# Gated linear attention and a mixture of experts on one core: the scans' additive operand in PSUM, the k product on GpSimd, one causal select in four by predicated copy, carried states without zero blocks

## The chip, the cores and the metric

The kernel runs on one core of a Trainium2 chip. Its engines are TensorE (PE in the profile; PEld is its weight load), VectorE (DVE), ScalarE (ACT), GpSimd (POOL) and SyncE (SP), which here issues most of the DMAs. The working memory is SBUF, 128 partitions wide; TensorE writes its products into PSUM, from which DVE and ACT read. The metric is the time of one execution on the device in microseconds; lower is better.

## The reference

Four sequences of 768 positions, with 8 heads of 48 channels, go through a gated linear attention in float32. Its output, 3072 tokens of 384 features, goes to a layer of 8 experts with a fixed capacity of 384 tokens each.

```python
# q, k, v, alpha: (4, 8, 768, 48), alpha in 0.8 .. 1.0
for t in range(S):
    state = alpha[:, :, t, :, None] * state + np.einsum('bhd,bhe->bhde', k[:, :, t], v[:, :, t])
    y[:, :, t] = np.einsum('bhd,bhde->bhe', q[:, :, t], state)
...
logits = x @ w_gate                      # x: y as (3072, 384)
order = np.argsort(-logits.flatten())    # greedy, at most cap = 384 tokens an expert
...
    h = np.maximum(x[mask] @ w1[e], 0.0)
    out[mask] = h @ w2[e]
```

## The kernel before

*Tiles.* The recurrence is computed in chunks of 128 positions, six to a sequence, 24 chunks in all. A step `s` of the attention loop takes four chunks (a group `g`) of one pair of heads (`p`); `s = 4*g + p`, so there are 24 steps, numbered 0 to 23. A tile has 128 partitions: rows 0 to 47 hold the channels of the first head, rows 64 to 111 those of the second. Along the free axis lie the four chunks `u` of 128 positions.

*One step.* DVE makes from the decays alpha two cumulative products with scans. Line 221 runs backwards through the step's four chunks: `sc[t] = alpha[t]*sc[t+1] + d1r[t]`. The alpha tile has a zero at each chunk's border (every 129th element), and `d1r` a one, so the product starts anew for each chunk. Line 222 takes the reciprocals of the four whole-chunk products into `d1f`, and line 224 scans forward with these as starting values: `ga`. Then `kh = k*sc` (line 229, DVE) and `qh = q*ga` (line 235, GpSimd). TensorE transposes `kh` (241) and ACT copies it as `kn` (243). The scores are `kh` against `qh`, for each chunk and head a matmul over the 64 rows of that head (250), into two PSUM tiles, `s0` and `s1`, with two buffers each. ACT copies each to SBUF (258), and GpSimd zeroes there what lies above the diagonal (259): two copies and two selects a step. TensorE forms the state that each chunk adds (269, PSUM bank `st`). The carry (273 to 289) goes chunk by chunk: ACT writes the state before the chunk, scaled by the chunk's decay, into a tile `sb` (282), and DVE adds the chunk's state (289), or copies it where a sequence begins (287). `sb` is block diagonal, 128x128: one 64x64 block for each head, the other two blocks zero from the beginning, and ACT writes one instruction for each block. The outputs are, for each chunk, one 128x128 matmul with `sb` (296) and two with the masked scores and v (302), all into the PSUM tile `y`. ACT copies it as `yt` (310). Two steps later the routing logits follow from it (315, also in the bank `st`), which DVE copies (318, where p is 0) or adds (320). With the last pair of a group comes a transpose and the table work of the first routing choice (`first_choice`, lines 347 to 365), a dozen small DVE instructions.

*The loop.* In iteration `s` the program names: the loads of step s+3, keys, scores and causal select of s, logits of s-2, states and carry of s, scans and products of s+2, outputs of s-1 and their copy. A scheduler then orders each engine's instructions. SP issues the loads of a step in a fixed order, alpha, k, q, v. Each of these has four buffers. The v tile of step s+3 takes the buffer of step s-1, which is free when the outputs of s-1 are done, and what stands behind that load on SP waits with it.

*After the attention* come the rest of the routing, a search for each expert's threshold by counting matmuls (551) and comparisons (503), gathers of each expert's tokens, and the two layers of each expert, each product in three terms of a split into two rounded parts (lines 719 to 789). The change does not touch their code.

```python
        if s + 2 < NS:
            decay(s + 2)
            scale_k(s + 2)
            scale_q(s + 2, nc.vector if s == 0 else nc.gpsimd)
        if s and s <= NS:
            mix(outputs(s - 1))
            emit(s - 1)
```

The first two steps are prepared before the loop by `first` (398), in halves.

## Time and profile before

| | us |
|---|---|
| three runs | 517.44, 517.86, 510.74; median 517.44 |
| the profiled execution, its own time | 513.45 |
| its span, first to last instruction | 511.7 |
| attention loop, from the first scan of the loop on (14 to 149) | 135 |
| end of the attention (149 to 160) | 11 |
| search for the thresholds of routing (160 to 200) | 40 |
| experts (200 to 511) | 311 |

| engine | busy us of the span | share |
|---|---|---|
| PE | 419.5 | 82% |
| DVE | 337.2 | 66% |
| POOL | 275.6 | 54% |
| ACT | 229.7 | 45% |

The mean clock granted to TensorE was 0.931 of full speed. Rows of groups read: line, engine, operation, output and inputs, shapes, count, then busy time in us and mean of one in ns, then the idle time of the engine just ahead of these instructions and what ended it. Rows of a stretch give the busy time of each engine in it with the number of instructions. Instructions of one engine overlap a little at their ends, so durations add up to somewhat more than busy time.

### The profile page before, as it was taken

The numbers are of one execution on the slowest core, as the hardware profiler recorded it, in microseconds if no ns is written. First come the engines' busy times: TensorE is split into PE (matmuls) and PEld (weight loads), VectorE is DVE, ScalarE is ACT, GpSimd is POOL, SyncE is SP. The second block draws the span as 40 slices with busy tenths as digits, with TensorE's granted clock in tenths as the row PEclk, the third lists the DMA queues.
The fourth block names the chain that finished last, engine by engine and source line by source line (L and its number), as shares of the span: only waits on it lengthen the run. The fifth ranks groups of instructions, "written<-read, shape, count | busy, mean of one in ns | idle before, by whom it ended". The sixth has DMA issues, their size and how long they took to land.

```text
span 511.7 us, 10469 instructions
## 1 busy us (share of the span) xinstructions
PE 419.5 (82%) x3982; PEld 365.8 (71%) x3982; DVE 337.2 (66%) x868; ACT 229.7 (45%) x524; POOL 275.6 (54%) x277
## 2 busy tenths in 40 slices
PE   6777877887878767985887867988967899999994
PEld 3555666666666646975786766877966789999994
DVE  7999897889743567687686796594684774121210
ACT  2676677677875433141322332242332245464521
POOL 2756755475630057274535455357548367978632
PEclk9999999889999957997988989897989899999998
DMA  8655556465503563170251161082152162620001
GB/s 257 206 169 174 168 164 169 162 176 176 167 1 122 216 205 122 44 252 0 83 212 46 51 243 47 1 277 63 60 188 94 30 217 68 250 91 26 31 17 46
DMA packets 44593, 65.17 MB, mean 127 GB/s; under 512 B 3328, under 2 KB 26880, under 8 KB 44544
## 3 DMA queue, kind: packets, MB, share of 16 engines
q1 hardware_dynamic: 38304, 50.35, 30.6%
q0 software_dynamic: 3072, 9.44, 5.7%
q10 hardware_dynamic: 3168, 4.72, 2.5%
q8 instruction: 31, 0.51, 0.4%
q14 instruction: 18, 0.15, 0.1%
HBM read 55.06 MB, written 9.44 MB: 126 GB/s over the span
## 4 chain that ended last, share of the span: by engine, by line
PE 44%; DVE 33%; DMA 9%; issue 6%; ACT 3%; POOL 1%; another core or an unknown queue 1%; SPq 1%; POOLq 0%; ACTq 0%; DVEq 0%
PE y L778 15%; PE h L758 14%; PE rt L551 5%; DVE sc L221 5%; DVE nd L563 4%; DVE cmp L503 4%; DMA al<-in_alpha_dram 4%; DVE ga L224 3%; PE xt L742 2%; DMA x_dram<-xg 2%; DMA raw_k<-in_k_dram 2%; PE y L302 1%; DVE st L289 1%; ACT sb L282 1%; PE y L296 1%
## 5 line engine op out<-in xcount | busy, mean ns | idle before, releaser
L724 POOL TENSOR_TENSOR wlo<-w1r,whi 128x384 fp32r<-128x384 f32 x64 | 71.2, 1115 | 85.7 <-ACT whi L719 85.4
L762 ACT ACTIVATE hh<-h 128x384 fp32r<-128x384 f32 x64 | 31.5, 492 | 107.6 <-PE h L758 105.3
L259 POOL TENSOR_SCALAR_AFFINE_SELECT sm<-sm 128x512 f32<-128x512 f32 x48 | 42.4, 902 | 59.8 <-ACT sm L258 59.8
L763 DVE SCALAR_TENSOR_TENSOR hl<-h,hh 128x384 fp32r<-128x384 f32 x64 | 35.4, 553 | 57.4 <-ACT hh L762 54.7
L778 PE MATMUL y<-whi,hh 128*128 128x384 f32 x192 | 70.3, 366 | 0.0
L778 PE MATMUL y<-wlo,hh 128*128 128x384 f32 x192 | 69.7, 363 | 0.0
L778 PE MATMUL y<-whi,hl 128*128 128x384 f32 x192 | 69.1, 361 | 0.0
L719 ACT ACTIVATE whi<-w1r 128x384 fp32r<-128x384 f32 x64 | 32.8, 522 | 80.0 <-PE y L778 69.5
L725 POOL TENSOR_TENSOR wlo<-w2r,whi 128x384 fp32r<-128x384 f32 x64 | 65.8, 1031 | 3.9 <-ACT whi L720 3.7
L282 ACT ACTIVATE sb<-st,sc 64x48 f32<-64x48 f32 x160 | 53.1, 332 | 29.5 <-DVE st L289 14.2
L699 POOL DMA_INDIRECT xr<-x_dram,idx x24 | 28.6, 1193 | 48.4 <-DVE val L630 31.2
L551 PE MATMUL rt<-o,cmp 128*128 128x8 bf16 x816 | 32.7, 175 | 25.0 <-DVE cmp L503 17.6
L551 PEld LDWEIGHTS <-cmp 128*128 128x128 bf16 x816 | 30.5, 118 | 31.7 <-DVE cmp L503 20.5
L758 PE MATMUL h<-xh,whi 128*128 128x384 f32 x192 | 48.1, 353 | 5.0 <-DVE hl L763 5.0
L758 PE MATMUL h<-xh,wlo 128*128 128x384 f32 x192 | 50.6, 363 | 0.0
L758 PE MATMUL h<-xl,whi 128*128 128x384 f32 x192 | 47.4, 349 | 0.0
L789 POOL DMA_INDIRECT out_dram<-yt,idx x24 | 24.5, 1022 | 28.5 <-ACT yt L782 23.0
L778 PEld LDWEIGHTS y<-whi,hl 128*128 128x128 f32 x192 | 39.0, 203 | 0.7 <-issue 0.6
L758 PEld LDWEIGHTS h<-xh,wlo 128*128 128x128 f32 x192 | 36.2, 200 | 4.6 <-issue 4.5
L758 PEld LDWEIGHTS h<-xh,whi 128*128 128x128 f32 x192 | 35.1, 195 | 6.1 <-DVE hl L763 5.6
L778 PEld LDWEIGHTS y<-wlo,hh 128*128 128x128 f32 x192 | 39.2, 204 | 0.1
L778 PEld LDWEIGHTS y<-whi,hh 128*128 128x128 f32 x192 | 39.1, 203 | 0.1
(169 smaller groups left out, 882.2 us busy)
## 6 DMA issues: line engine op xcount, KB each, us to landing
w1r<-in_moe_w_dram SPq DMA_DIRECT2D x16, 768.0 KB, 4.8
w2r<-in_moe_w_dram SPq DMA_DIRECT2D x16, 768.0 KB, 7.6
al<-in_alpha_dram SPq DMA_DIRECT2D x24, 256.0 KB, 3.3
raw_k<-in_k_dram SPq DMA_DIRECT2D x24, 256.0 KB, 4.2
raw_q<-in_q_dram SPq DMA_DIRECT2D x24, 256.0 KB, 4.2
vt<-in_v_dram SPq DMA_DIRECT2D x24, 256.0 KB, 2.7
x_dram<-xg ACTq DMA_DIRECT2D x6, 768.0 KB, 3.5
xr<-x_dram,idx POOLq DMA_INDIRECT x24
```

The source lines that it names most:

```text
L221: nc.vector.tensor_tensor_scan(sc[:, ::-1], a[:, ::-1], d1r[:, ::-1], 1.0, op0=OP.mult, op1=OP.add)
L259: nc.gpsimd.affine_select(SM[s][:, h], SM[s][:, h], pattern=[[0, 4], [1, C]], compare_op=OP.is_ge, fill=0.0, base=0, channel_multiplier=-1)
L282: nc.scalar.activation(SB[s, u][hs, h, :D], St[p][hs], AF.Copy, scale=ac[hs])
L551: nc.tensor.matmul(cnt, cmp[:, j // U, :, j % U], o[:, j], start=(j == 0), stop=(j == NU - 1))
L699: last_gather[0] = nc.gpsimd.indirect_dma_start(out=XR[i][:, b], out_offset=None, in_=x_dram, in_offset=bass.IndirectOffsetOnAxis(ap=IDX[i ...
L719: nc.scalar.activation(hi[:, 0], a, AF.Copy)
L724: nc.gpsimd.tensor_sub(lo[:, 0], a, hi[:, 0])
L725: nc.gpsimd.tensor_sub(lo[:, 1], c, hi[:, 1])
L758: nc.tensor.matmul(o, a[:, 0, d], x[:, d], start=(n == 0), stop=(n == 3 * DB - 1))
L762: nc.scalar.activation(hh, o, AF.Relu)
L763: nc.vector.scalar_tensor_tensor(hl, o, 0.0, hh, op0=OP.max, op1=OP.subtract)
L778: F2[i, q] = nc.tensor.matmul(Y[b], a[:, bs], w[:, 1].rearrange("p a b -> p (a b)"), start=(q == 0 and n == 0), stop=(q == FB - 1 and n == 2))
```

## The change

The scans' additive operands, `d1r` and `d1f` in SBUF, are replaced by one PSUM tile, `aux`, of 1024 columns: the whole-chunk reciprocals stand in its first part, the backward scan reads ones at every 129th element further up. Both scans are one element shorter (516), and a helper `scans` serves the loop and the first two steps. To make room in PSUM, the scores have two tiles in place of four. The k product moves from DVE to GpSimd. In odd steps the second head's select is one DVE instruction, a copy from PSUM under a mask into a tile that is zero where the mask is, so that ACT's copy and GpSimd's select go; the masked scores lie in two fixed tiles. The carried state `sb` has 64 columns, both heads below each other, written by one ACT instruction; TensorE reads it with two 64x64 matmuls. The copy of a sequence's first state and the first copy of the logits move from DVE to ACT.

```diff
-    d1r = ap_.tile([128, W4], F32)
-    d1f = ap_.tile([128, W4], F32)
...
+    aux = ps.tile([128, 1024], F32, name="aux")
+    nc.vector.memset(aux[:, :W4 + 3 * 129], 0.0)
+    nc.vector.memset(aux[:, W4 - 1:W4 + 3 * 129:129], 1.0)
     nc.vector.memset(wg, 0.0)
+
+    tril = ap_.tile([128, C], I32)
+    trif = ap_.tile([128, C], F32)
+    nc.gpsimd.memset(trif, 1.0)
+    nc.gpsimd.affine_select(trif, trif, pattern=[[1, C]], compare_op=OP.is_ge, fill=0.0, base=0,
+                            channel_multiplier=-1)
+    nc.gpsimd.tensor_copy(tril, trif)
+    SMT = [ap_.tile([128, 2, 4, C], F32, name=f"sm{i}") for i in range(2)]
+    for t in SMT:
+        nc.gpsimd.memset(t[:, 1], 0.0)
...
-    SBT = [[ap_.tile([128, 2, 64], F32, name=f"sb{i}{u}") for u in range(4)] for i in range(2)]
+    SBT = [[ap_.tile([128, 64], F32, name=f"sb{i}{u}") for u in range(4)] for i in range(2)]
...
     def decay(s):
         a = raw["a", s]
-        sc = work.tile([128, W4], F32, name="sc", bufs=4)
-        nc.vector.tensor_tensor_scan(sc[:, ::-1], a[:, ::-1], d1r[:, ::-1], 1.0, op0=OP.mult, op1=OP.add)
-        nc.vector.reciprocal(d1f[:, 0:W4 - 1:129], sc[:, 1:W4:129])
-        ga = work.tile([128, W4], F32, name="ga", bufs=3)
-        nc.vector.tensor_tensor_scan(ga, a, d1f, 1.0, op0=OP.mult, op1=OP.add)
-        SC[s], GA[s] = sc, ga
+        sc = SC[s] = work.tile([128, W4], F32, name="sc", bufs=4)
+        ga = GA[s] = work.tile([128, W4], F32, name="ga", bufs=3)
+        scans(a, sc, ga, 0, 4)
+
+    def scans(a, sc, ga, u, n):
+        lo, hi, top = 129 * u, 129 * (u + n), W4 + 3 * 129
+        nc.vector.tensor_tensor_scan(sc[:, lo + 1:hi + 1][:, ::-1], a[:, lo + 1:hi + 1][:, ::-1],
+                                     aux[:, top - 129 * n:top][:, ::-1], 1.0, op0=OP.mult, op1=OP.add)
+        nc.vector.reciprocal(aux[:, lo:hi:129], sc[:, lo + 1:hi + 1:129])
+        nc.vector.tensor_tensor_scan(ga[:, lo:hi], a[:, lo:hi], aux[:, lo:hi], 1.0, op0=OP.mult, op1=OP.add)
 
     def scale_k(s):
         KH[s] = work.tile([128, 4, C], F32, name="kh", bufs=3)
-        nc.vector.tensor_mul(KH[s], raw["k", s],
+        nc.gpsimd.tensor_mul(KH[s], raw["k", s],
...
     def scores(s):
-        o = [ps.tile([128, 4, C], F32, name=f"s{h}", bufs=2) for h in range(2)]
+        o = [ps.tile([128, 4, C], F32, name="s", bufs=2) for h in range(2)]
...
     def causal(s):
         o = SM[s]
-        SM[s] = work.tile([128, 2, 4, C], F32, name="sm")
+        SM[s] = SMT[s % 2]
         for h in range(2):
+            if h and s % 2:
+                nc.vector.copy_predicated(SM[s][:, h], tril[:, None, :].to_broadcast([128, 4, C]), o[h])
+                continue
             nc.scalar.activation(SM[s][:, h], o[h], AF.Copy)
...
             if c:
                 SB[s, u] = SBT[s % 2][u]
-                for h in range(2):
-                    hs = slice(64 * h, 64 * h + 64)
-                    nc.scalar.activation(SB[s, u][hs, h, :D], St[p][hs], AF.Copy, scale=ac[hs])
+                nc.scalar.activation(SB[s, u][:, :D], St[p], AF.Copy, scale=ac)
...
             if c == 0:
-                nc.vector.tensor_copy(St[p], stp[:, u])
+                nc.scalar.activation(St[p], stp[:, u], AF.Copy)
...
         for u in us:
-            yield lambda u=u: nc.tensor.matmul(
-                o[:, u], SB[s, u].rearrange("p h d -> p (h d)"), QH[s][:, u],
-                start=(u == us[0]), stop=False, skip_group_check=True)
+            for h in range(2):
+                hs = slice(64 * h, 64 * h + 64)
+                yield lambda u=u, hs=hs: nc.tensor.matmul(
+                    o[hs, u], SB[s, u][hs], QH[s][hs, u],
+                    start=(u == us[0]), stop=False, skip_group_check=True)
...
         if p == 0:
-            nc.vector.tensor_copy(lt, ltp)
+            nc.scalar.activation(lt, ltp, AF.Copy)
```

In `first` the two scans of a half now follow each other, and the two products come behind them; before, the k product stood between the scans.

The change also moves instructions. On DVE, in the middle of the loop where step 13 is prepared, stood from one addition of the logits (`lt`) to the next the following; numbers behind names are those of single tiles, and scans are listed as SCALAR_TENSOR_TENSOR on 517 columns:

```order
L320 TENSOR_TENSOR lt0_172<-lt0_172,st_176 128x128
L221 SCALAR_TENSOR_TENSOR sc_1269<-al2_123,d1r_127 128x517
L289 SCALAR_TENSOR_TENSOR st3_1177<-st3_850,sc_1027,st_176 128x48
L222 RECIPROCAL d1f_128<-sc_1269 128x4
L229 TENSOR_TENSOR kh_1274<-raw_k_1136,sc_1269 128x512
L289 SCALAR_TENSOR_TENSOR st3_1181<-st3_1177,sc_1027,st_176 128x48
L224 SCALAR_TENSOR_TENSOR ga_1272<-al2_123,d1f_128 128x517
L289 SCALAR_TENSOR_TENSOR st3_1185<-st3_1181,sc_1027,st_176 128x48
L320 TENSOR_TENSOR lt0_172<-lt0_172,st_176 128x128
```

The same place on DVE in the changed kernel, whose lines 234, 236 and 237 are the scans and the reciprocal, 302 the carry, 335 the logits' addition:

```order
L271 COPY_PREDICATED sm1_158<-tril_152,s_1137 128x512
L335 TENSOR_TENSOR lt0_179<-lt0_179,st_183 128x128
L234 SCALAR_TENSOR_TENSOR sc_1250<-al2_123,aux_148 128x516
L302 SCALAR_TENSOR_TENSOR st3_1161<-st3_839,sc_1011,st_183 128x48
L236 RECIPROCAL aux_148<-sc_1250 128x4
L302 SCALAR_TENSOR_TENSOR st3_1164<-st3_1161,sc_1011,st_183 128x48
L237 SCALAR_TENSOR_TENSOR ga_1251<-al2_123,aux_148 128x516
L302 SCALAR_TENSOR_TENSOR st3_1167<-st3_1164,sc_1011,st_183 128x48
L335 TENSOR_TENSOR lt0_179<-lt0_179,st_183 128x128
```

The k product is gone from between the carries; the first scan of a step ahead still stands ahead of the running step's carries, and the predicated copy of an odd step ahead of the logits' addition.

On POOL, the selects and products of the same steps before:

```order
L235 TENSOR_TENSOR qh_1118<-raw_q_956,ga_1114 128x512
L259 AFFINE_SELECT sm_1159<-sm_1159 128x512 x2
L235 TENSOR_TENSOR qh_1196<-raw_q_1054,ga_1192 128x512
L259 AFFINE_SELECT sm_1237<-sm_1237 128x512 x2
L235 TENSOR_TENSOR qh_1276<-raw_q_1138,ga_1272 128x512
```

And on POOL now, where 241 is the k product, 247 the q product and 274 the select:

```order
L241 TENSOR_TENSOR kh_1175<-raw_k_1040,sc_1170 128x512
L274 AFFINE_SELECT sm1_158<-sm1_158 128x512
L247 TENSOR_TENSOR qh_1177<-raw_q_1042,ga_1171 128x512
L241 TENSOR_TENSOR kh_1255<-raw_k_1123,sc_1250 128x512
L274 AFFINE_SELECT sm0_157<-sm0_157 128x512 x2
L247 TENSOR_TENSOR qh_1257<-raw_q_1125,ga_1251 128x512
```

A k product of a step ahead now stands in front of the select of the running step, and the selects alternate between one and two.

On PE, the carried-state matmuls and the outputs of one step before; names with `st` are states, `xt` and the score matmuls follow behind:

```order
L296 MATMUL y_1198<-qh_937,sb00_156 128x128
L296 MATMUL y_1198<-qh_937,sb01_157 128x128
L296 MATMUL y_1198<-qh_937,sb02_158 128x128
L269 MATMUL st_176<-vt_880,kn_1147 48x48 x6
L296 MATMUL y_1198<-qh_937,sb03_159 128x128
L302 MATMUL y_1198<-sm_1075,vt_804 48x128 x8
```

And on PE now, where 311 is the carried state, 284 the states and 317 the masked scores against v:

```order
L330 MATMUL st_183<-yt_1120,wg_69 32x128 x4
L311 MATMUL y_1179<-qh_924,sb00_163 64x128 x2
L311 MATMUL y_1179<-qh_924,sb01_164 64x128 x2
L311 MATMUL y_1179<-qh_924,sb02_165 64x128 x2
L311 MATMUL y_1179<-qh_924,sb03_166 64x128
L284 MATMUL st_183<-vt_872,kn_1134 48x48 x6
L311 MATMUL y_1179<-qh_924,sb03_166 64x128
L317 MATMUL y_1179<-sm0_157,vt_798 48x128 x8
```

Four matmuls over all 128 rows have become eight over 64 rows each, in pairs for one chunk, with the states of the next step still among the last of them.

More of the change, by code (lines that the diff above doesn't have):

```diff
@@ L190, in gla_moe_kernel @@
                 load_v(i)
-    nc.vector.memset(d1r, 0.0)
-    nc.vector.memset(d1r[:, 0:W4:129], 1.0)
-    nc.vector.memset(d1f, 0.0)
+    aux = ps.tile([128, 1024], F32, name="aux")
+    nc.vector.memset(aux[:, :W4 + 3 * 129], 0.0)
+    nc.vector.memset(aux[:, W4 - 1:W4 + 3 * 129:129], 1.0)
     nc.vector.memset(wg, 0.0)
+    tril = ap_.tile([128, C], I32)
[7 more added lines that the diff above has]
+        nc.gpsimd.memset(t[:, 1], 0.0)
     for h in range(2):
@@ L403, in first @@
         qh = QH[s] = work.tile([128, 4, C], F32, name="qh", bufs=3)
-        for u, rs in ((0, slice(0, 259)), (2, slice(259, W4))):
+        for u in (0, 2):
             us = slice(u, u + 2)
-            fs = slice(129 * u, 129 * u + 258)
-            nc.vector.tensor_tensor_scan(sc[:, rs][:, ::-1], a[:, rs][:, ::-1], d1r[:, rs][:, ::-1], 1.0,
-                                         op0=OP.mult, op1=OP.add)
-            nc.vector.reciprocal(d1f[:, fs][:, 0:258:129], sc[:, fs][:, 1:258:129])
+            scans(a, sc, ga, u, 2)
             nc.vector.tensor_mul(kh[:, us], raw["k", s][:, us],
@@ L412, in first @@
                                          ap=[list(sc.ap[0]), [129, 2], [1, C]]))
-            nc.vector.tensor_tensor_scan(ga[:, fs], a[:, fs], d1f[:, fs], 1.0, op0=OP.mult, op1=OP.add)
             nc.vector.tensor_mul(qh[:, us], raw["q", s][:, us],
-                                 ga[:, fs].rearrange("p (g x) -> p g x", x=129)[:, :, 1:])
+                                 ga[:, 129 * u:129 * u + 258].rearrange("p (g x) -> p g x", x=129)[:, :, 1:])
     spin(WARM_UP)
```

## The prediction

> **What bounds the kernel now.** First the view by stretches, cut where the attention loop's DVE work begins, at its end, at the route search's end and at the span's end.
>
> ```profile
> core 0: us, PE busy (x) PEld busy (x) DVE busy (x) ACT busy (x) POOL busy (x), PEclk, DMA share, GB/s
> 14.00:149.00 135.00, 106.28 (x1427) 84.27 (x1423) 116.75 (x262) 97.83 (x238) 82.46 (x80) 0.97 0.54 161
> 200.00:511.00 311.00, 265.65 (x2092) 246.17 (x2090) 181.09 (x467) 104.52 (x225) 172.28 (x163) 0.92 0.30 100
> ...
> 27.42 1.16 PE L250 MATMUL s<-qh,kh 64*128 64x128 f32 x16
> ...
> 148.93 1.16 PE L250 MATMUL s<-qh,kh 64*128 64x128 f32 x16
> ```
>
> The two timeline rows are the score matmuls of step 3 and of step 23: 20 intervals in 121.51 us, 6.08 us a step. The first stretch is 135/6.08 = 22.2 steps long, so a step holds 5.26 us of DVE, 4.79 of PE, 4.41 of ACT and 3.71 of POOL. DVE is the tightest, PE half a microsecond behind it. The FFN stretch is bound by PE, and the change does not edit its code; all that is to be had lies in the attention.
>
> Next the groups of DVE, POOL and ACT in 14 to 158 us, and the spread of the same instructions.
>
> ```profile
> L224 DVE TENSOR_TENSOR_SCAN ga<-al,d1f 128x517 f32<-128x517 f32 x22 | 31.4, 1428 | 0.0
> L221 DVE TENSOR_TENSOR_SCAN sc<-al,d1r 128x517 f32<-128x517 f32 x22 | 30.9, 1405 | 4.9 <-DMA al<-in_alpha_dram 4.6 <-ACT sb L282 0.2
> L229 DVE TENSOR_TENSOR kh<-raw_k,sc 128x512 f32<-128x512 f32 x22 | 22.1, 1006 | 0.4 <-DMA raw_k<-in_k_dram 0.3
> L320 DVE TENSOR_TENSOR lt<-lt,st 128x128 f32<-128x128 f32 x17 | 4.8, 282 | 10.6 <-PE st L315 10.6
> ...
> L259 POOL TENSOR_SCALAR_AFFINE_SELECT sm<-sm 128x512 f32<-128x512 f32 x46 | 40.7, 903 | 50.9 <-ACT sm L258 50.9
> L282 ACT ACTIVATE sb<-st,sc 64x48 f32<-64x48 f32 x160 | 53.1, 332 | 29.5 <-DVE st L289 14.2 <-DVE d1f L222 5.0 <-DVE st L287 3.3
> ...
> L224 DVE TENSOR_TENSOR_SCAN ga<-al,d1f x22: 1222/1227/2047, 16.8 to 136.6; 128x517 f32<-128x517 f32 x22
> L229 DVE TENSOR_TENSOR kh<-raw_k,sc x22: 656/842/1715, 16.0 to 135.6; 128x512 f32<-128x512 f32 x22
> L235 POOL TENSOR_TENSOR qh<-raw_q,ga x21: 1175/1643/2129, 23.2 to 141.0; 128x512 f32<-128x512 f32 x21
> ```
>
> Scans and the k product take (31.4+30.9+22.1)/22 = 3.84 us of a step. The same scan takes 1222 ns or up to 2047 (least, median, most), the GpSimd product 1175 to 2129, the k product 656 to 1715: DVE and GpSimd slow each other when both read two SBUF operands. Last the chain that ends last, and the SP queue's waits.
>
> ```profile
> 106.91 1.76 PE y L302 x16
> ...
> 108.68 0.33 SPq L182
> ...
> 109.10 3.10 DMA al<-in_alpha_dram
> ...
> 112.32 1.42 DVE sc L221
> ...
> 114.38 4.65 DMA raw_k<-in_k_dram
> ...
> 119.05 0.70 DVE kh L229
> ...
> 119.76 0.10 DVE m L351
> ...
> 123.01 0.42 DVE cmp L364
> ...
> SPq L182 <- PE y L302: 73.2, 19, 6.5
> ...
> DMA to landing us min/median/max: 3.1/3.3/6.0
> ```
>
> The v load of step s+3 takes the buffer that the output matmuls of step s-1 free. It waited 19 times, and the alpha load of s+4 stands behind it on SP: outputs, v issue, alpha load, scan. The last row is the alpha loads' landing. Between 119.76 and 123.43 stands the first-choice table work that every fourth step adds to DVE: eleven instructions, about 2 us of the chain without the scan and the carries among them.
>
> **The change part by part.**
>
> *Scans.* Their additive operand lies in PSUM, so a scan has one SBUF input. I take the uncontended 1.22 us (one element shorter changes nothing): 2×1.22 = 2.44 in place of 62.3/22 = 2.83, a gain of 0.39 a step. What a PSUM operand costs a scan no row shows. The nearest rows are L320 above and this one, also with a PSUM operand:
>
> ```profile
> L763 DVE SCALAR_TENSOR_TENSOR hl<-h,hh 128x384 fp32r<-128x384 f32 x64 | 35.4, 553 | 57.4 <-ACT hh L762 54.7
> ```
>
> (553-282)/(384-128) = 1.06 ns an element, against 1222/517 = 2.36 of the scan: a PSUM stream is quicker than the scan takes elements, so 1.22 is nearest. The upper end is both in turn, 1222 + 516×1.06 = 1.77 us; below 1.2 nothing speaks for it.
>
> GpSimd's selects, and the ACT copies ahead of them, cost in undisturbed places:
>
> ```profile
> 139.79 1.22 POOL L259 TENSOR_SCALAR_AFFINE_SELECT sm<-sm 128x512 f32<-128x512 f32 x2 [0.78 <-ACT sm L258]
> ...
> 151.11 1.09 ACT L258 ACTIVATE sm<-s 128x512 f32<-128x512 f32 x2
> ```
>
> *The k product* leaves DVE: 1.00 us a step off. On GpSimd it takes what the q product takes, 1.18 us at least, 2.13 at most; I take 1.18, since the scans no longer read two SBUF operands. GpSimd then has 1.18+1.18+1.5 selects×0.61 = 3.3 us: not the bound. The product stands in GpSimd's queue ahead of the select of the running step, so a late k load now also holds the select, and through it the outputs; in the chain above k landed 4.65 us after its issue, but the first scan must come before it anyway. The product ends 0.3 us later than DVE's median of 842, two steps before the transposes need it: nothing.
>
> *The select by predicated copy*, every second step one 128x512: by 1.06 ns an element plus some 0.15 fixed, 0.69 us; as slow as a scan it would be 1.22. I take 0.69, 0.34 a step. It removes one copy of 0.55 us from ACT and one select from GpSimd. It stands ahead of the logits' addition on DVE, and nothing of PE's next step but the logits waits for that.
>
> *Carried state*: 80 instead of 160 ACT instructions of 332 ns, 26.6 us of ACT busy time, 1.2 a step; ACT then holds about 3.4 us, even with the two kinds of copies in the last rows below moved to it. The first-chunk copy may there stand behind a copy of 0.55 us, and the next carry on DVE and with it the logits wait for it: at most 0.55 in 8 of 24 steps, 0.2 a step; 0 taken, as ACT has 40% idle. Each 128x128 matmul becomes two of 64x64 in opposite corners. Score matmuls already run in pairs of 64 rows:
>
> ```profile
> 131.02 1.16 PE L250 MATMUL s<-qh,kh 64*128 64x128 f32 x16
> 133.56 0.43 PE L315 MATMUL st<-yt,wg 128*32 128x128 f32 x8 [1.38 <-ACT yt L310]
> ...
> 156.04 1.16 PE L296 MATMUL y<-qh,sb 128*128 128x128 f32 x8
> ...
> L315 PE MATMUL st<-yt,wg 128*32 128x128 f32 x168 | 8.9, 283 | 20.5 <-ACT yt L310 8.2 <-DVE st L289 6.2 <-DVE iota L132 2.2
> ...
> L287 DVE COPY st<-st 128x48 f32<-128x48 f32 x16 | 3.1, 192 | 1.3 <-PE st L269 1.2
> L318 DVE COPY lt<-st 128x128 f32<-128x128 f32 x6 | 1.7, 280 | 2.1 <-PE st L315 2.1
> ```
>
> Eight half-row score matmuls took 1.16 us, as long as four full carried-state matmuls (each matmul has two records), so if the halves of a pair overlap, nothing changes: I take 0, and no gain, since as many columns stream as before. The upper end is no overlap: one matmul costs 0.29, there are 80 more over 22 steps, 0.29×80/22 = 1.05 us a step.
>
> On exactly this the Trainium skill, in TensorEngine Tiling (Array Packing), § Restrictions and Gotchas, speaks against the change: different row tiles, it says, cannot access the same PSUM bank at the same time. The score pairs write two tiles, the new pairs one y tile, so no row here tests it; by it the term would be the upper end, by the score rows 0.
>
> *Fewer score tiles* (two rather than four): step 23's scores begin at 148.93 and the copies that empty both tiles end at 152.20, 3.3 us later, where the next scores need them after 5. No cost, with over a microsecond of slack.
>
> *Setup*: GpSimd fills the mask and half of two mask-product tiles before the loop. Its first k product is due when DVE's was, at 16.0 us, and the fills are covered by the first alpha and k loads until then; without that cover the first step waits once, by less than the product's 1.18 us. None taken. The routing and FFN instructions are the same, and some move by a few places in PE's queue: 0, ±3 us, about the size of one wait there; a gain is as likely as a loss.
>
> **The sum.** DVE: 5.26 - 0.39 - 1.00 + 0.34 - about 0.1 for the moved copies (4.8 us of durations over 22 steps, half of each beside its neighbours) = 4.1 us a step. PE stays at 4.79 and becomes the tightest. What PE waited, 135-106.28 = 28.7 us or 1.29 a step, is mostly the row L315 (20.5). Its part behind DVE shrinks.
>
> ```profile
> L289 DVE SCALAR_TENSOR_TENSOR st<-st,sc,st 128x48 f32<-128x48 f32 x64 | 16.0, 249 | 1.5 <-PE st L269 1.1
> L222 DVE RECIPROCAL d1f<-sc 128x4 f32<-128x4 f32 x22 | 3.8, 173 | 0.1
> ...
> 135.09 1.05 PE L302 MATMUL y<-sm,vt 128*48 128x128 f32 x16
> 136.06 0.66 PE L241 MATMUL xt<-ident,kh 128*128 128x128 f32 x4
> ```
>
> From states to logits DVE must now run a carry, the reciprocal, a carry, one scan and a carry, 0.25+0.17+0.25+1.22+0.25 = 2.1 us by single durations and some 0.15 of starting, against 1.05+0.66+1.16 = 2.9 us of output, transpose and score matmuls on PE, of which the outputs partly run among the states: 1.8 to 2.9. I leave 0.5 us a step: 0.1 of the chain, and 0.4 for the five steps of 22 that also hold the first-choice table work, 2 us of DVE each. That gives 5.3.
>
> The load loop allows it: outputs to alpha's issue 0.43, landing 3.3, start 0.12, scan 1.22, then from the reciprocal to the last carry 2.0 (0.17+0.25+1.22+0.25 and a start), and PE from logits to the end of the outputs 2.6 (133.56 to 136.14 in the rows above): 9.7 us for two steps, 4.85 a step. So 5.3 us a step: 0.78 saved, over 21 steps 16.4 us. After the last decay the tail's three blocks of scaled states are halved:
>
> ```profile
> 142.45 2.12 ACT L282 ACTIVATE sb<-st,sc 64x48 f32<-64x48 f32 x6 [1.53 <-DVE chu L359]
> ...
> 152.89 2.12 ACT L282 ACTIVATE sb<-st,sc 64x48 f32<-64x48 f32 x6 [0.69 <-DVE st L289]
> 155.68 0.42 PE L315 MATMUL st<-yt,wg 128*32 128x128 f32 x8 [0.75 <-ACT yt L310]
> ```
>
> 1.06 us for each of the three, limited by PE's own wait in the later ones: 2.5 together. Total gain 18.9 us. The profiled execution took 513.45 us (span 511.7), so 494.6; the median of the three runs is 517.44, 4 above it, and I set the forecast midway between the two bases: 496.5.
>
> **The rivals.** *The loads are the bound (0.10).* The al row's maximum is 6.0. If alpha lands 5.2 after its issue on average, since a quicker loop asks for more than 161 GB/s and the four loads of a step meet, the loop takes 11.6 for two steps, 5.8 each: gain 5.9+2.5, some 507. Against it: the median is 3.3.
>
> *The half matmuls do not overlap (0.09).* PE 4.79+1.05 = 5.84 and a little waiting, 5.9: gain 3.8+2.5, some 509. For it speaks that both halves write one tile; this is the rule cited above.
>
> *Contention stays (0.06).* If a scan with one SBUF input still collides with GpSimd, now busier, GpSimd holds 2×2.13+1.5×1.2 = 6.06 us a step and becomes the bound: some 512, no change. For it: GpSimd runs two products where it ran one. Against it: in the timelines every scan over 1.3 us ran beside a q product or a select of GpSimd, and what DVE read beside them was two SBUF operands, which this change ends for the scans. The Trainium skill, SBUF — State Buffer, § Who interferes with whom, states that a DVE instruction with at most one SBUF input does not contend with GpSimd; no run here shows it yet.
>
> *The scan is slow from PSUM (0.07), the one that ends slower.* If PSUM halves its rate, 2.44 us each, DVE holds 4.1+2.44 = 6.5 busy and, with the 0.4 of waits that no order removes, 6.9 a step: 0.86×21 = 18 us lost, less the tail's 2.5, some 531. It breaks even where a scan takes 2.0 us and is over 2% slower from about 2.3. Against it: the 1.06 ns an element of L763.
>
> **How the numbers follow.** The main case has 0.68, its own range 487 (a step of 4.85, PE without waits) to 506 (5.75: scans at 1.4, predicated copy at 1.22 and first-choice steps in full). The range must leave out at most 2 in 10: up to 510 it takes in the loads and most of the half matmuls. Differences within 2% are about what a measurement of this kernel tells from no change; faster by over 2% of 517.44 means below 507.1. The main case gives 0.68 faster; loads, half matmuls and contention 0.25 within 2%; the slow scan 0.07 slower.
>
> **What would show it.** Both scans near 1.22 us with no spread, the k product on GpSimd below 1.3, the predicated copy near 0.7, score starts 5.3 us apart, eight carried-state matmuls within about 1.16 us, L315's counterpart waiting about a third as long. It is wrong if a scan is over 1.5 us, if the half matmuls take 2 us a step, if alpha's wait grows to over 0.5 us a step, or if the FFN stretch changes by more than 3 us.

## The result, and the profile after

| | before | after |
|---|---|---|
| median of the runs, us | 517.65 (510.74 to 520.68, 4 runs) | 491.14 (488.81 to 493.06, 4 runs) |
| ratio, 95% interval | | 0.9528 (0.942 to 0.9637) |
| profiled execution, span, us | 513.45, 511.7 | 488.81, 487.1 |

Ratios leave out executions that took over 1.5% longer than the fastest of the same kernel; medians include them.

Where the 24.6 us of the two profiled spans went, by marks on TensorE:

| stretch | before | after | difference |
|---|---|---|---|
| start to the scores of step 3 | 27.4 | 24.4 | -3.0 |
| scores of step 3 to scores of step 23 (20 intervals) | 121.5 | 110.6 | -10.9 |
| to the first counting matmul of the routing search | 17.2 | 14.9 | -2.3 |
| to the first expert matmul | 25.9 | 27.2 | +1.3 |
| first to last expert matmul | 312.3 | 302.6 | -9.7 |
| rest | 7.4 | 7.4 | 0 |

Two rows of this table came out far from the forecast: the start, and above all the experts, whose code the change leaves alone. First the stretches of the changed kernel, with the columns of the prediction's first view: the start, the 20 intervals, the experts; behind them the score matmuls that bound the intervals.

```profile
core 0: us, PE busy (x) PEld busy (x) DVE busy (x) ACT busy (x) POOL busy (x), PEclk, DMA share, GB/s
14.00:24.40 10.40, 8.43 (x129) 6.29 (x128) 10.33 (x19) 6.24 (x18) 9.00 (x17) 1.00 0.59 195
24.42:134.99 110.57, 97.35 (x1431) 74.28 (x1430) 81.00 (x209) 58.36 (x156) 68.19 (x74) 1.00 0.59 176
177.10:479.70 302.60, 270.97 (x2133) 251.57 (x2133) 184.21 (x473) 107.07 (x231) 180.77 (x168) 0.92 0.32 106
...
24.42 1.16 PE L262 MATMUL s<-qh,kh 64*128 64x128 f32 x16
...
134.99 1.16 PE L262 MATMUL s<-qh,kh 64*128 64x128 f32 x16
```

A step takes 110.57/20 = 5.53 us. It holds 4.05 us of DVE, 4.87 of PE, 2.9 of ACT and 3.4 of POOL: PE is now the busiest. In the start DVE is busy 10.33 of 10.40 us, and in the same stretch of before it was, too:

```profile
14.00:27.40 13.40, 10.20 (x128) 7.42 (x124) 13.36 (x26) 9.17 (x22) 10.16 (x17) 1.00 0.56 178
```

So the first steps are bound by DVE outright, and what DVE no longer does is saved there in full. Now the groups of DVE and POOL in 14 to 146 us, and for scans and k product the least, median and largest duration.

```profile
L237 DVE TENSOR_TENSOR_SCAN ga<-al,aux 128x516 f32<-128x516 f32 x22 | 27.0, 1226 | 1.1
L234 DVE TENSOR_TENSOR_SCAN sc<-al,aux 128x516 f32<-128x516 f32 x22 | 26.9, 1225 | 19.5 <-DMA al<-in_alpha_dram 18.7 <-ACT sb L295 0.5 <-ACT sm L273 0.2
L271 DVE COPY_PREDICATED sm<-tril,s 128x512 f32<-128x512 int32 x12 | 8.9, 740 | 2.9 <-PE s L262 2.8
...
L241 POOL TENSOR_TENSOR kh<-raw_k,sc 128x512 f32<-128x512 f32 x22 | 26.0, 1184 | 9.6 <-DVE sc L234 3.8 <-DVE L L345 2.5 <-DMA raw_k<-in_k_dram 1.8
L247 POOL TENSOR_TENSOR qh<-raw_q,ga 128x512 f32<-128x512 f32 x21 | 24.8, 1181 | 4.6 <-PE y L311 3.7 <-issue 0.7
...
L237 DVE TENSOR_TENSOR_SCAN ga<-al,aux x26: 691/1228/1230, 5.4 to 123.7; 128x516 f32<-128x516 f32 x22, 128x258 f32<-128x258 f32 x4
...
L241 POOL TENSOR_TENSOR kh<-raw_k,sc x22: 1175/1184/1192, 14.5 to 124.0; 128x512 f32<-128x512 f32 x22
...
DMA to landing us min/median/max: 3.1/3.6/5.2
```

The spread is gone: no scan takes over 1.23 us, no product over 1.192. DVE's waits have moved to the alpha load, 4.6 us before and 18.7 now. The last row is the landing of the alpha loads: their median rose only from 3.3 to 3.6 us, so it is not the loads themselves that have become slow. On PE, the groups in the 20 intervals, and one place where all eight half matmuls of a step run together:

```profile
L262 PE MATMUL s<-qh,kh 64*128 64x128 f32 x321 | 23.6, 285 | 0.0
L311 PE MATMUL y<-qh,sb 64*64 64x128 f32 x264 | 23.0, 280 | 0.0
...
L284 PE MATMUL st<-vt,kn 128*48 128x48 f32 x260 | 10.9, 213 | 6.4 <-DVE cnt L396 2.4 <-issue 2.2 <-DVE L L345 1.2
L330 PE MATMUL st<-yt,wg 128*32 128x128 f32 x160 | 8.5, 283 | 6.3 <-DVE st L302 3.0 <-ACT kn L255 3.0
...
140.39 1.09 PE L311 MATMUL y<-qh,sb 64*64 64x128 f32 x16
```

Of what PE still waits, 13.2 us in 20 steps, nearly all stands ahead of the states and the logits. In the expert stretch the waits of PE are, in the changed kernel (engine and what waited for whom; us in total, times, longest):

```profile
PE rt L562 <- DVE cmp L514: 16.1, 10, 6.5
PE rt L562 <- DVE o L651: 5.6, 2, 3.1
PE xt L753 <- DVE xl L758: 2.6, 1, 2.6
PE rt L668 <- DVE rts L666: 2.5, 1, 2.5
PE rt L599 <- DVE rts L598: 2.5, 2, 1.2
PE h L769 <- DVE hl L774: 1.9, 2, 1.3
```

and were before:

```profile
PE rt L551 <- DVE cmp L503: 17.6, 7, 6.3
PE rt L551 <- DVE o L640: 7.5, 3, 4.1
PE rt L588 <- DVE rts L587: 5.4, 4, 1.7
PE h L758 <- DVE hl L763: 5.0, 2, 4.0
PE rt L558 <- DVE g L552: 4.9, 3, 3.5
```

The stretch as a whole was before:

```profile
192.02:504.34 312.32, 270.09 (x2138) 250.47 (x2136) 188.09 (x474) 105.87 (x228) 178.25 (x168) 0.92 0.30 103
```

PE is busy as long in both (270.1 and 271.0 us); the rows of waits sum to 40.4 us before and 31.2 now, as far apart as the stretches. The same instructions, in another order, wait less for each other. Most of these waits stand ahead of `rt`, the small matmuls of the routing, whose later rounds run among the experts' matmuls: 36.5 us before and 27.1 now. So the name "experts" for this stretch hides where it is won.

### The profile page after: what moved, and what is told of

It is laid out like the page before. It is cut to its first block, busy times and chain, and to the rows that moved or that the text cites. A ratio compares the mean times of both kernels' runs of the same rounds, so it can differ in the third digit from the quotient of the medians.

```text
span 487.1 us, 10728 instructions
## 1 busy us (share of the span) xinstructions
PE 420.1 (86%) x4142; PEld 363.5 (75%) x4142; DVE 309.6 (64%) x835; ACT 193.9 (40%) x454; POOL 274.1 (56%) x292
## 4 chain that ended last, share of the span: by engine, by line
PE 46%; DVE 30%; DMA 14%; issue 5%; ACT 2%; POOL 2%; POOLq 0%; DVEq 0%; ACTq 0%; SPq 0%
PE h L769 16%; PE y L789 14%; DMA al<-in_alpha_dram 11%; PE rt L562 6%; DVE cmp L514 5%; DVE sc L234 4%; DVE nd L574 4%; DVE ga L237 3%; DMA x_dram<-xg 2%; PE y L311 1%; PE y L317 1%; PE xt L354 1%; PE xt L753 1%; PE xt L703 1%; DVE hl L774 1%
## 5 line engine op out<-in xcount | busy, mean ns | idle before, releaser
L735 POOL TENSOR_TENSOR wlo<-w1r,whi 128x384 fp32r<-128x384 f32 x64 | 67.8, 1063 | 83.2 <-ACT whi L730 82.9
L736 POOL TENSOR_TENSOR wlo<-w2r,whi 128x384 fp32r<-128x384 f32 x64 | 68.9, 1082 | 0.8 <-ACT whi L731 0.5
L789 PE MATMUL y<-wlo,hh 128*128 128x384 f32 x192 | 68.4, 356 | 0.0
L710 POOL DMA_INDIRECT xr<-x_dram,idx x24 | 31.0, 1290 | 41.2 <-DVE val L641 31.3
L769 PE MATMUL h<-xh,whi 128*128 128x384 f32 x192 | 51.0, 370 | 1.9 <-DVE hl L774 1.9
L769 PE MATMUL h<-xl,whi 128*128 128x384 f32 x192 | 49.1, 360 | 0.0
L274 POOL TENSOR_SCALAR_AFFINE_SELECT sm<-sm 128x512 f32<-128x512 f32 x36 | 22.4, 637 | 38.4 <-ACT sm L273 38.4
L234 DVE TENSOR_TENSOR_SCAN sc<-al,aux 128x516 f32<-128x516 f32 (+1 forms) x26 | 29.7, 1142 | 21.0 <-DMA al<-in_alpha_dram 20.2
L295 ACT ACTIVATE sb<-st,sc 128x48 f32<-128x48 f32 x80 | 25.9, 333 | 35.2 <-DVE st L302 23.4
L769 PEld LDWEIGHTS h<-xh,whi 128*128 128x128 f32 x192 | 37.0, 206 | 3.1 <-DVE hl L774 2.5
```

Source lines behind the costliest of these rows:

```text
L234: nc.vector.tensor_tensor_scan(sc[:, lo + 1:hi + 1][:, ::-1], a[:, lo + 1:hi + 1][:, ::-1], aux[:, top - 129 * n:top][:, ::-1], 1.0, op0=O ...
L295: nc.scalar.activation(SB[s, u][:, :D], St[p], AF.Copy, scale=ac)
L710: last_gather[0] = nc.gpsimd.indirect_dma_start(out=XR[i][:, b], out_offset=None, in_=x_dram, in_offset=bass.IndirectOffsetOnAxis(ap=IDX[i ...
L735: nc.gpsimd.tensor_sub(lo[:, 0], a, hi[:, 0])
L736: nc.gpsimd.tensor_sub(lo[:, 1], c, hi[:, 1])
L769: nc.tensor.matmul(o, a[:, 0, d], x[:, d], start=(n == 0), stop=(n == 3 * DB - 1))
```

## The experiments

Each experiment is the changed kernel with one edit, except the second, the ninth and the twelfth, which start from the kernel before. The scheduler orders an edited kernel anew, and so every one is compared by its stretches. Each group of experiments has its own runs of before beside it (median 512.90 for 1 to 4, 512.21 for 5 to 8, 516.85 for 9 to 11), so kernels of different groups are compared by their ratios. From the first counting matmul on, the instructions of PE, DVE, ACT and GpSimd stand in one of two orders, by their names and shapes in the traces, which do not keep the numbers of single buffers: experiments 1, 2, 3, 5, 6, 8, 11 and 12 have the order of before, 4, 7, 9 and 10 that of the changed kernel. The expectations speak of a third order, that of experiments 1, 3 and 4; by the traces 1 and 3 have that of before and 4 has that of the changed kernel.

**1. Six v buffers in the changed kernel.** Does the load ring (outputs, v load, alpha load queued behind it) hold the loop?

```diff
-        VT[s] = work.tile([128, 4, 2, 64], F32, name="vt", bufs=RB)
+        VT[s] = work.tile([128, 4, 2, 64], F32, name="vt", bufs=RB + 2)
```

> The changed kernel with six buffers for the v tiles in place of four, nothing else. Theory: the loop (5.53 us a step, score start to score start, steps 3 to 23) is now held by the ring outputs, v load, alpha load queued behind it, scan. With two more v buffers the alpha loads go out two steps earlier: DVE's 20.2 us of waiting for alpha fall below 3 us, the step falls to about 5.1 us (PE's 4.87 us busy a step and a little waiting), the loop's 20 intervals lose 7 to 10 us. Rival: PE's own chain holds the step, and the waits for alpha are slack; then the 20 intervals change by less than 2 us. The routing and expert rows stand in another order in this kernel than in the changed one, so the loop is compared by the score starts.

Measured: 503.49 us, ratio to before 0.9845 (0.9751 to 0.9939), slower than the changed kernel; step 5.76 us. The alpha waits did go, and another one came. The two rows are DVE's waits for alpha in the whole attention, and its waits for a free `sc` tile in 27 to 135 us:

```profile
  DMA al<-in_alpha_dram: 1.4, 1
...
DVE sc L234 <- ACT sb L295: 7.5, 11, 2.2
```

On DVE, between 28 and 135 us, the two scans of a step stand together ahead of the carries in 16 steps of this kernel, in 9 of the changed kernel; in the others a carry or two stand between them. Eleven times the first scan waited for a tile that ACT's scaled states of an older step still read, with the carries queued behind it. Theory and rival both miss. As the order of DVE changed with the edit, this run does not tell whether the alpha waits held the loop. Of the 13.0 us between this profiled span and the changed kernel's, 8.5 lie in the expert stretch (311.1 us, in the order of before) and 4.7 in the intervals.

**2. The same in the kernel before.** The same edit.

> The kernel before with six buffers for the v tiles, nothing else; routing and expert rows in the order of before. Theory: DVE bounds that loop (5.26 of 6.08 us busy, 4.6 us of waits for alpha in all), so the 20 intervals of 121.5 us lose at most 5 us. Rival: the loads held that loop as well, and the change gained by moving them; then the intervals lose over 8 us. The time from the first expert matmul to the end stays at 312.7 us within 3 us if it depends on the order of the instructions alone.

Measured: 528.99 us, ratio 1.0312 (1.0175 to 1.0449): slower than before, which neither side expected. Step 7.02 us. The stretch of its 20 intervals, and DVE's waits there:

```profile
26.54:166.97 140.43, 110.17 (x1298) 85.94 (x1297) 103.43 (x237) 88.33 (x217) 72.99 (x63) 0.88 0.39 123
...
DVE sc L221 <- ACT sb L282: 19.8, 14, 2.3
```

The same stretch of the kernel before was:

```profile
27.42:148.93 121.51, 96.00 (x1299) 76.78 (x1298) 103.36 (x237) 88.57 (x217) 72.30 (x63) 0.97 0.54 159
```

DVE's work is that of before (103.4 us), and the same wait for `sc` tiles has taken the place of alpha. But PE's busy time rose from 96.0 to 110.2 us for the same matmuls, at a granted clock of 0.88 in place of 0.97. That is 14 of the 18.9 us that the intervals grew, and is taken up in the last section. The expert stretch was 306.8 us, in the order of before, 5.5 less than there: more than the 3 us that the expectation allows, so the order alone does not fix this time.

**3. The scans' operand back in SBUF.**

```diff
-    aux = ps.tile([128, 1024], F32, name="aux")
+    aux = ap_.tile([128, 1024], F32, name="aux")
```

> The changed kernel with the scans' additive operand in an SBUF tile, nothing else. Theory: with two SBUF operands the scans collide with the GpSimd products again: scans 1.4 to 1.6 us in the mean (1.226 now, none over 1.23), GpSimd products 1.6 us and more in the mean (1.18 now), GpSimd at 5 us or more a step, the step 5.9 to 6.2 us, the 20 intervals 8 to 13 us longer than the 110.6 of the changed kernel. Rival: the operand's place matters little, since DVE waits 20 us for alpha anyway; the scans grow into that slack and the intervals stay within 3 us.

Measured: 519.45 us, ratio to before 1.011 (1.0 to 1.022); the changed kernel's whole gain is gone. Step 6.53 us. The scans' groups, and the stretch of the intervals:

```profile
L237 DVE TENSOR_TENSOR_SCAN ga<-al,aux 128x516 f32<-128x516 f32 x22 | 38.0, 1729 | 1.0
L234 DVE TENSOR_TENSOR_SCAN sc<-al,aux 128x516 f32<-128x516 f32 x22 | 31.7, 1441 | 14.8 <-DMA al<-in_alpha_dram 14.8
...
32.47:163.07 130.60, 107.10 (x1431) 82.18 (x1430) 93.97 (x205) 59.25 (x155) 80.49 (x71) 0.91 0.50 148
```

Contention is shown: most of this kernel's attention rows stand where they stood, and the scans take 1.44 and 1.73 us in the mean, the GpSimd products 1.42 and 1.54. The intervals lost 20 us, more than the 8 to 13 of the theory; 9.8 of them are PE's busy time (107.1 against 97.4) at a lower clock. GpSimd is at 4.0 us a step, not at the 5 expected, so it did not become the bound; that the lengthened chain did it is likely and not shown. Of the 31.9 us between the profiled spans 20.0 are the intervals', 8.1 the start's and 4.6 the expert stretch's, which is in the order of before; the search gave 0.7 back. The start ran at half clock from 9 to 32 us, with PE busy all the time from 14 us on; no run shows whether the operand or chance began that spell.

**4. The k product back on DVE.**

```diff
-        nc.gpsimd.tensor_mul(KH[s], raw["k", s],
+        nc.vector.tensor_mul(KH[s], raw["k", s],
```

> The changed kernel with the k product on DVE in the loop, nothing else. Theory: the product comes back with 0.66 to 1.0 us a step on DVE, the slower when it runs beside the q product on GpSimd; DVE has 0.9 us a step of waits for alpha, but the scan behind each product belongs to the chain from alpha to the carries, so about half of it shows: 0.3 to 0.6 us a step, the 20 intervals 6 to 12 us longer. The scans stay at 1.226 us. Rival: it disappears in the waits for alpha, less than 3 us. Second rival: DVE is the bound again at once, 1.0 us a step, 20 us.

Measured: 497.28 us, ratio 0.9716 (0.962 to 0.9813). Step 5.88 us, 0.35 more, 7.1 us in 20 intervals, as the theory had it; 2.1 of them are PE's busy time, at a mean clock of 0.97. The product took 809 ns in the mean, the scans stayed at 1.22, DVE's waits for alpha fell to 13 us. The expert stretch was 306.2 us in the order of the changed kernel, the longest with that order; its PE was busy for 275.2 us at a clock of 0.90, against 271.0 at 0.92.

**5. Six `sc` buffers.** This leaves all attention rows, up to the last scores, in the order of the changed kernel and puts the rows behind them in the order of before.

```diff
-        sc = SC[s] = work.tile([128, W4], F32, name="sc", bufs=4)
+        sc = SC[s] = work.tile([128, W4], F32, name="sc", bufs=6)
```

> The changed kernel with six buffers for the tile sc in place of four. Its attention rows stand in exactly the order of the changed kernel on all engines; its routing and expert rows stand in the order of the first, third and fourth experiments. It is there for the 9.7 us by which the stretch from the first expert matmul to the last fell (312.3 before, 302.6 after), which the prediction had not. Theory: the order of those rows made it; then this kernel keeps the step of 5.5 us and the expert stretch is 306 us or more, as in the three experiments with the same order (311.1, 307.3, 306.2). Rival: the stretch differs from execution to execution whatever the order; then it is as likely to be near 303 here, and the median stays within 2 us of 491.

Measured: 497.34 us, ratio 0.9735 (0.9658 to 0.9813). The two stretches:

```profile
25.23:136.65 111.42, 97.04 (x1430) 74.16 (x1430) 80.83 (x209) 58.51 (x156) 67.92 (x74) 1.00 0.56 175
178.00:488.10 310.10, 272.40 (x2136) 253.15 (x2135) 190.18 (x474) 106.18 (x228) 176.92 (x168) 0.91 0.31 104
```

The attention is the changed kernel's (5.57 us a step), and the expert stretch takes 310.1 where that one has 302.6. The ratio is 0.9735, against 0.9528 of the changed kernel and 0.9577 of the seventh experiment, which has that kernel's order and ran in the same group. The theory holds.

**6. Six v and six `sc` buffers**, both edits above.

> The changed kernel with six buffers for v and six for sc. With six v buffers alone the waits for alpha went (20.2 to 1.4 us), but the scans, pulled ahead, waited for a free sc tile (11 waits on ACT's scaled states, 7.5 us) and the step took 5.76 us. Theory: the ring through the v load holds the changed kernel's loop, and the sc tiles held the first experiment's; with both free the step falls to 5.0 to 5.2 us, DVE's waits for alpha and for sc tiles under 3 us together. Rival: PE and the chain through logits hold the loop; the step stays between 5.4 and 5.8 us.

Measured: 498.48 us, ratio 0.9761 (0.9676 to 0.9845); step 5.63 us, alpha waits 10.8 us. The theory falls: with the alpha waits halved and no wait for `sc` tiles, PE still waited 12.8 us in the intervals, 13.2 in the changed kernel. Expert stretch 305.4, in the order of before.

**7. The two copies back on DVE.**

```diff
-                nc.scalar.activation(St[p], stp[:, u], AF.Copy)
+                nc.vector.tensor_copy(St[p], stp[:, u])
...
-            nc.scalar.activation(lt, ltp, AF.Copy)
+            nc.vector.tensor_copy(lt, ltp)
```

> The changed kernel with the copy of a sequence's first state and the first logits copy on DVE again. Its routing and expert rows stand in the order of the changed kernel. Theory: 16 and 6 instructions of 0.2 and 0.28 us come back to an engine that waits 0.9 us a step: step 5.5 to 5.6 us, median within 2 us of 491; the expert stretch 302.6 within 2 us if its order decides. Rival: ACT's copy had shortened the chain to the carries; then 0.2 us a step, 4 us in all.

Measured: 493.74 us, ratio 0.9577 (0.9496 to 0.9658), no difference from the changed kernel that these runs can tell. Step 5.70 in the profile, above the theory's 5.6; of the 3.5 us that its intervals are longer, 3.0 are PE's busy time (100.38 us, clock 0.97). The expert stretch, in the changed kernel's order:

```profile
183.30:485.90 302.60, 270.84 (x2133) 251.48 (x2133) 184.28 (x473) 107.12 (x231) 180.62 (x168) 0.92 0.31 106
```

302.6 us once more.

**8. The block-diagonal state**: two ACT instructions and one full matmul for each chunk, as before.

```diff
-                nc.scalar.activation(SB[s, u][:, :D], St[p], AF.Copy, scale=ac)
+                for h in range(2):
+                    hs = slice(64 * h, 64 * h + 64)
+                    nc.scalar.activation(SB[s, u][hs, h, :D], St[p][hs], AF.Copy, scale=ac[hs])
...
+            yield lambda u=u: nc.tensor.matmul(
+                o[:, u], SB[s, u].rearrange("p h d -> p (h d)"), QH[s][:, u],
+                start=(u == us[0]), stop=False, skip_group_check=True)
```

> The changed kernel with the carried state as a 128x128 block-diagonal tile again: two ACT instructions of 0.33 us for each chunk, one full matmul. Theory: the half matmuls overlap in pairs, so PE's busy time a step stays within 0.1 us of 4.87; ACT gains 1.2 us a step, and since ACT waits for the carries' chain in most steps and the logits wait behind it, the step grows by 0.1 to 0.3 us, and the tail after the last score matmuls (7.2 us to the last output matmul) by 1 to 2 us. Rival: the halves run one after the other (0.29 us each, 1.05 us a step); then PE's busy time falls by about 1 us a step here and the step with it.

Measured: 505.31 us, ratio 0.9848 (0.9764 to 0.9931). Step 5.82 us (0.29 more), and from the last scores to the last output matmul 8.5 us instead of 7.2. The group of full matmuls in the 20 intervals:

```profile
L311 PE MATMUL y<-qh,sb 128*128 128x128 f32 x132 | 23.7, 312 | 0.6 <-ACT sb L297 0.4
```

66 full matmuls take 23.7 us here, at a mean clock of 0.96 in the intervals, and 132 halves (two records each) 23.0 in the changed kernel at 1.00. At full clock in both, the eight halves of a step took 1.09 us in the row shown above, four full ones 1.16 in the prediction's rows. So the halves overlap, and the rival is out. The growth of the step stands in three intervals of 8.2 to 8.6 us that hold a spell at half clock each; the other 17 take 5.37 us in the mean, and the same ones 5.44 in the changed kernel. So the wait for ACT, on which the theory rests, is not shown to lengthen a step by itself. The expert stretch was 315.1, in the order of before, so 12.5 of the 18.6 us between its profiled span and the changed kernel's are not the state's. Against the fifth experiment, which shares that order and was measured in the same group, the median is 8.0 us higher.

**9. One part alone: the kernel before with the operand in PSUM**, by the `scans` of the changed kernel and two score tiles; all else as before.

> The kernel before with one part of the change: the scans' additive operand in PSUM, and the two score tiles that this leaves room for. The k product stays on DVE, the selects and the carried state as before. Theory: the scans fall from 1.42 us in the mean to 1.22 to 1.23 without spread, which is 0.39 us of DVE a step; DVE still bounds the loop, so the step falls from 6.08 by 0.2 to 0.4 us, the 20 intervals by 4 to 8 us. Rival: what DVE gains goes into the waits for logits and loads (23 us of waits on DVE in the loop of before); then the step stays above 6.0 us. The rows after the attention stand in an order of their own.

Measured: 500.06 us, ratio 0.9671 (0.9622 to 0.972). The scans took 1226 and 1217 ns. The intervals fell by 3.6 us, to 5.89 a step, and by 5.3 us against the second profile of before (twelfth experiment). One of them, from 135.19 to 144.04, holds a spell at half clock; the 19 at full clock have 5.74 in the mean, the 17 of before that are at full clock 5.97. The expert stretch was 302.0, in the order of the changed kernel, so about 10 of the 13.2 us between the profiled spans lie there.

**10. All selects on ACT and GpSimd.**

```diff
-            if h and s % 2:
+            if False:
```

> The changed kernel without the predicated copy: all selects as ACT copy and GpSimd select. GpSimd gets 0.32 us a step more (3.4 in all), ACT 0.3, DVE loses 0.37. Theory: none of the three bounds the loop, which PE and the table work of the first choice hold; the step stays within 5.4 to 5.7 us. Rival: the select of odd steps was the last that the outputs wait for; then the step grows by 0.3 us or more.

Measured: 492.54 us, ratio 0.9512 (0.9441 to 0.9583); step 5.57, expert stretch 302.9 in the order of the changed kernel. The predicated copy moves nothing that can be measured.

**11. The table work of groups 0 to 3 in one pass**, at group 3.

```diff
-            first_choice(g)
+            if g >= BATCH - 1:
+                first_choice(range(BATCH) if g == BATCH - 1 else [g])
```

> The changed kernel with the table work of the first routing choice done once for groups 0 to 3, at the end of group 3, rather than after each group; groups 4 and 5 as before. In the changed kernel the intervals from score start to score start are 4.78 us in the mean into a step with s%4=0 and 5.95 into those with 2 and 3, where the table work stands. Theory: this work, about 2 us on DVE in a chain with TensorE, holds the loop above PE's 4.87 us; without it the intervals of steps 6 to 15 fall to 4.8 to 5.1 us in the mean (5.5 now), the 20 intervals lose 4 to 8 us, and the pass of group 3 costs 1 to 2 us more than one did. Rival: another wait takes its place, the loads' ring first of all; then steps 6 to 15 stay above 5.3 us.

Measured: 501.47 us, ratio 0.9692 (0.9632 to 0.9751). From the scores of step 5 to those of step 15 it took 5.50 us a step; the changed kernel has 5.81 there, not the 5.5 that the expectation says. So three passes fewer saved 0.3 us a step there. DVE's waits for alpha rose from 20.2 us in the whole attention to these, in us and times:

```profile
  DVE sc L235: 23.0, 15
```

The step stayed above 5.3 us, as the rival had it; that the load ring took over is not shown by a rise of 2.8 us. The other intervals, with the pass of group 3 and two spells at half clock, gave the gain back (step 5.68 over all), and the expert stretch was 312.6, in the order of before.

**12. The kernel before once more.**

> The kernel before once more, unchanged, for a second profile. Theory: the order of the rows after the attention decides most of the expert stretch, and half-clock spells the rest; its stretch from the first expert matmul to the last lies between 306 and 313 us (312.3 and, with six v buffers, 306.8 so far) and not near the 302.6 that the changed kernel and its seventh experiment showed. Rival: it varies at will, and can be 303 here.

Measured, in one execution: 508.78 us; step 6.16, expert stretch 305.8. The theory named 306 as the lower end, missed by 0.2. All fourteen profiles, by their order:

| order | expert stretch, us | mean |
|---|---|---|
| of before (before, 1, 2, 3, 5, 6, 8, 11, 12) | 312.3, 311.1, 306.8, 307.2, 310.1, 305.4, 315.1, 312.6, 305.8 | 309.6 |
| of the changed kernel (changed, 4, 7, 9, 10) | 302.6, 306.2, 302.6, 302.0, 302.9 | 303.3 |

The means are 6.3 us apart; the ranges overlap only between 305.4 and 306.2. Within one order up to 10 us are left that the order does not explain; part of it is the clock, as in the fourth experiment.

## Why the prediction came out right

The forecast was 496.5 us, clearly faster than before; the median is 491.14. Against the profiled execution of before it had a gain of 18.9 us, and 24.6 were measured.

- *DVE's load.* From 5.26 to 4.1 us a step was forecast, 4.05 measured. Scans, k product and GpSimd's 3.4 us are as the sum had them; the predicated copy took 0.74 us for 0.69. The third experiment shows that it is the operand's place that does it: with the k product on GpSimd and the operand in SBUF the scans take 1.44 and 1.73 us, and the step is 6.53 us, worse than before. The operand alone gave 0.19 to 0.27 us a step, by the first and the second profile of before (ninth), the k product 0.35 (fourth), the carried state 0.29 with half-clock spells in it (eighth). These sum to more than the 0.55 that the step lost: they were measured on different kernels, and how the gain divides stays open. The prediction reads its first rows as a contention of two SBUF operands on either side; GpSimd's select has only one, and the 15 scans of before that ran beside a select but no product took 1.35 us in the mean, the 13 beside neither 1.22. The Trainium skill's rule cited for this rival, in SBUF — State Buffer, § Who interferes with whom, agrees with the trace: of the changed kernel's 43 scans that begin after 14 us, 39 ran beside a GpSimd product, and none took over 1.23 us.
- *The half matmuls* cost nothing: eight took 1.09 us together, where four full ones took 1.16. The rule of the Trainium skill that the prediction cites from TensorEngine Tiling (Array Packing), § Restrictions and Gotchas, is not what the trace shows here: the halves of a pair wrote one PSUM tile and overlapped.
- *The step*, 5.3 forecast, 5.53 measured. The terms that were mis-sized: PE's work, 4.79 taken and 4.87 measured, and the waits of PE, 0.5 taken and 0.66 measured. The forecast called the load ring an allowance of 4.85; DVE's waits for alpha, named as a sign of error if over 0.5 us a step, came to 0.9. What of this bounds the step was not settled: with alpha's waits removed, in another order (first), or halved (sixth), the step did not fall; the table work thinned out (eleventh) gave 0.3 us where it was thinned out. A kernel that lifts both was not run.
- *The start* was counted as one more interval, 0.78 us, and gave 3.0, since DVE fills it wholly. Together with the loop 13.9 us came of the 16.4 forecast.
- *The tail*: 2.5 forecast, 2.3 measured to the first counting matmul. The eighth experiment, which puts the two ACT instructions back, loses 1.3 us there and so supports the mechanism.
- *The experts.* "The routing and FFN instructions are the same, and some move by a few places in PE's queue: 0, ±3 us" is the step that failed. The expert stretch took 9.7 us less, and the search ahead of it 1.3 more. The prediction set the size by one wait; the waits ahead of the routing's small matmuls alone changed by 9.4 us. That the order does it is shown by the fifth experiment (same attention order, other order behind it, 7.5 us more in the stretch), by the ninth (the kernel before with one part of the change, drawing the changed kernel's order: 302.0 us) and by the means of the two orders, 6.3 us apart. The rest of the 9.7 us is the spread within an order: the profiled execution of before was among the long ones of its own. This part of the gain is luck and no merit of the edit's idea: of the nine variants of the changed kernel six drew the order of before again.
- *The rivals.* The slow scan and lasting contention are excluded by the scans' rows, the half matmuls by the eighth experiment. The rival of the loads had alpha landing after 5.2 us on average; the longest landing took 5.2, the median 3.6. That the ring through them holds the loop in part is not excluded.

So the sign was right, and the mechanism was right for the attention: DVE's load fell as summed, and PE became the busiest. Two of the prediction's own signs of being wrong came all the same, alpha's wait over 0.5 us a step and the expert stretch off by more than 3 us. The gain of start and loop was forecast 2.5 us too high and the rest 8 us too low; that the total lies within 6 us of the forecast is in part luck, since the errors have opposite signs.

## What to carry to other kernels

A second operand moved into PSUM can be worth more than the time it saves on its own engine, when that operand slows another engine beside it: here its move is what let GpSimd take a second product at full speed. Where a scheduler orders the program, an edit in one stage reorders the next, and one or two percent can come from there; mark the stages and compare them one by one, with a variant that changes only the later order. And a wait that stands in the profile with 20 us is not yet a bound: one experiment took it away, another halved it, and neither gained in the loop.

## What the runs showed of the hardware that was not expected

TensorE's clock often falls to half for some microseconds after a pause of about 2 us, and so a loop that waits more can also compute more slowly. The second profile of before shows it, in the stretches ahead of, in and behind a pause, and in the first matmuls after it (2.61 us is the pause):

```profile
84.00:88.00 4.00, 4.00 (x63) 3.19 (x60) 1.38 (x4) 2.64 (x6) 2.93 (x4) 1.00 0.80 256
88.00:92.00 4.00, 1.47 (x20) 1.11 (x18) 3.89 (x8) 2.77 (x7) 1.60 (x1) 0.94 0.67 217
92.00:98.00 6.00, 5.93 (x51) 4.86 (x51) 3.64 (x14) 2.77 (x7) 3.68 (x3) 0.50 0.10 36
98.00:102.00 4.00, 4.00 (x66) 3.33 (x66) 3.52 (x11) 3.57 (x10) 0.67 (x1) 0.96 0.77 251
...
92.07 0.65 PE L315 MATMUL st<-yt,wg 128*32 128x128 f32 x8 [2.61 <-DVE st L289]
```

Eight logits records take 0.65 us there against 0.43 elsewhere. Over the 14 profiles, between 20 and 150 us, 39 pauses of PE lasted 1.60 us or more, and after 25 of them the granted clock was below 1 in the stretch from 0.5 to 2 us behind the pause; of the 60 pauses between 1.0 and 1.6 us it was so after 3. Which pause is followed by a spell is not shown; their length alone does not decide it. The Trainium skill, TensorE: Matmul & The Clock Gate, § HAM oscillation — how this bites in real kernels, warns of idle gaps above some 3.4 us; here shorter ones came ahead of the spells. The longest pause of the changed kernel in that part is 1.38 us, and its clock stayed at 1.00. Before, it was 0.97 over the intervals, and in the second experiment 0.88, where PE's busy time grew by 14 us. So a part of the loop's gain may be a clock that no longer falls; no run isolates how large it is.
